# Two attentions on one core: the loads and splits of B's projection weights put in a set order, and B's gates loaded and made later

## The chip, the core and the metric

The kernel runs on one core of a Trainium2 chip. A core has five engines with instruction queues of their own: TensorE (PE, matrix products into PSUM), VectorE (DVE), ScalarE (ACT), GpSimd (POOL, which also issues DMAs) and SyncE (SP, which here only issues DMAs). Each engine works through its queue in order, and an instruction that waits holds up all behind it. Sixteen DMA engines move data. The time is the device time of the whole program in microseconds.

## What is computed

Two independent attentions over 2048 positions of 576 features, with 32 heads of 18, side by side in the output.

```python
# A: all heads share one k and one v
q = split_heads(x @ wq); k = x @ wk; v = x @ wv
a = merge(softmax(q @ k.T * 18**-0.5) @ v) @ wo

# B: four segments of 512, each causal within itself, plus a memory of the earlier ones
q, k, v = (split_heads(x @ w) for w in (wq, wk, wv))
g = sigmoid(beta)                       # one gate per head
for s in range(4):
    a_dot = softmax(causal(q[s] @ k[s].T * 18**-0.5)) @ v[s]
    a_mem = (phi(q[s]) @ M) / (phi(q[s]) @ z + 1e-6)      # phi(t) = t + 1 if t > 0 else exp(t)
    o[s] = g * a_mem + (1 - g) * a_dot
    M += phi(k[s]).T @ v[s]; z += phi(k[s]).sum()
b = merge(o) @ wo
```

## The kernel before

**Two stages.** The first (lines 146 to 558) makes all projections and writes q, k, v and the shifts of the softmax to DRAM. Then follows a branch on a flag (line 561), which all engines pass together. The second stage (from line 627) loops over the heads: scores, exponentials, products with v, output projection. Its order is written out by hand. The diff touches the first stage alone.

**Products in parts.** Every operand of a projection is split into a rounded high part and a remainder: `split_w` rounds a piece of raw weights `wr` into `wh` on ScalarE (L207) and subtracts on another engine to get `wl` (L208). For x the pair is L194 and L197/L198, mostly on VectorE. A projection (`proj`, L222) is 14 matmuls over five slices k of the 576 features: three products each for k = 0 to 3, two for k = 4, which holds only 64 features, loaded twice into both halves of the partitions (so its load is two DMAs).

**A's projections.** Four chunks c of 512 positions (L234), in each five tiles t in the order 4, 0, 1, 2, 3. Tile 4 holds the last heads' q, the shared k and v. For each tile, after its matmuls: for tile 4 a reduction km (DVE, L279), a copy vT of v's rows (ACT, L281), and four transposes by PE (L284); then for all tiles the magnitude AQ (ACT, L286), a split of the result into `qp` (ACT cast L111, DVE subtraction L112; three buffers), and a store to DRAM (SP). Beside it one tile of the next chunk's x is split (`nx[2](t)`; its raw tile `xr` has three buffers, loaded by SP), and, in chunks 2 and 3, one piece of B's weights is loaded and split (`load_wk`, L210).

**B's weights** come in 15 pieces of 128 rows. Five pieces of 648 columns (v's first half and part of k), five of 576 columns (the rest of k and v) and five of 504 columns (q of heads 0 to 27). The first ten are traced in A's chunks 2 and 3, the last five in the first loop of B's segment 0 (L430). Their targets `wBh` and `wBl` take the memory that held the raw x and weights of A's first chunks, so they can be written only when these have been read. Raw pieces stand in `wr`: two buffers in pool `pt`, and two in pool `p1`, which ends with A's part (L351).

**B's segments.** For each of four segments s: five tiles (L412) with projection, reduction kmB (L420), split (L111, L112), store, and, except in the last segment, a feature map `phi` (two ACT instructions L363 and L364, then DVE L366) that PE transposes (`natural`, L393); then the values (L454; ACT copies them to `vch` and issues their stores), then four tiles of q (L492). In segment 0 the projection of the first tile is made ahead (`ahead`, L329), before A's last small products. PE first needs the 504-column pieces at L492.

**The order on each engine** in this stage is laid at compile time by a planner. It follows the text of the program, except that it puts work ahead that it reckons to be ready sooner, by its own estimates of durations. `tc.issue_after(i)` queues what follows behind instruction i of the same engine. `tc.keep_in_program_order(i)`, used after the change, queues i behind the instruction of its engine that stands just ahead of it in the text. Neither waits for anything by itself.

**Gates and masks.** In chunk 2 (L303 to L325) POOL issues six small loads of masks, a store of ones and seven loads that spread beta over partitions; ACT and DVE make the gate `gt` and `omg` = 1 - gate from them. `gt` is first read in segment 1 (L408), `omg` in the second stage (L684), `sel` and `hmask` at L335 and L339.

Of the kernel before, what the change touches and what calls it, by code (L numbers as in the profile page):

```python
# [7 lines left out]
F32 = mybir.dt.float32  # L8
# [3 lines left out]
AF = mybir.ActivationFunctionType  # L12
ALU = mybir.AluOpType
# [55 lines left out]
def attention_pair_kernel(ctx, tc, a_xT, a_w, a_wo, b_xT, b_w, b_wo, b_beta, ident_d, hmask_d, bmask_d, cmask_d, sel_d, zmask_d, selx_d, sely_d, out):  # L69
# [76 lines left out]
    with ExitStack() as ph:  # L146
# [23 lines left out]
        def halves(k):  # L170
# [2 lines left out]
                return [(slice(0, 128), slice(128 * k, 128 * k + 128))]  # L173
            return [(slice(0, 64), slice(512, 576)), (slice(64, 128), slice(512, 576))]


        raw = [pw.tile([128, 5, 3 * D], F32, name=n) for n in ("wBl", "wBh")]
        XRAW = [(raw[0], CA), (raw[0], CA + C), (raw[1], 0)]

        def load_part(dst, w, c0, n, k, queue):  # L180
            for rows, src in halves(k):
                queue.dma_start(dst[rows], w[src, c0 : c0 + n])
# [5 lines left out]
        def load_xk(xh, xl, xT, c, k):  # L188
            if xT is a_xT and c < 3:
                xr = xraw(c, k)  # L190
            else:
                xr = px.tile([128, C], F32, name="xr", bufs=3)
                load_part(xr, xT, c * C, C, k, nc.sync)
            (nc.scalar.copy if xT is a_xT and c == 0 else nc.vector.tensor_copy)(xh[:, k], xr)  # L194
            engine = nc.gpsimd if xT is a_xT and (c, k) == (1, 3) else nc.vector
            if k < 4:
                return engine.tensor_tensor(xl[:, k], xr, xh[:, k].bitcast(F32), op=ALU.subtract)  # L197
            engine.tensor_tensor(xh[64:128, k], xr[64:128], xh[64:128, k].bitcast(F32), op=ALU.subtract)  # L198

        def next_x(xT, c):  # L200

# [3 lines left out]

        def split_w(wh, wl, wr, c0, n, k, engine):
            nc.scalar.copy(wh[:, k, c0 : c0 + n], wr)  # L207
            return engine.tensor_tensor(wl[:, k, c0 : c0 + n], wr, wh[:, k, c0 : c0 + n].bitcast(F32), op=ALU.subtract)  # L208
# [18 lines left out]
        wAl = p1.tile([128, 5, CA], F32R, name="wAl")  # L227


        TILES = (4, 0, 1, 2, 3)  # L230
        AQ = p1.tile([128, 5, S], BF, name="AQ")
        km = p1.tile([128, 4], F32, name="km")
        kAp = p1.tile([128, 1], F32, name="kAp")
        for c in range(NCH):  # L234
            ready = {}
            if c == 0:

                for k in range(5):
                    load_part(raw[0][:, k, :CA], a_w, 0, CA, k, nc.sync)
                    load_part(xraw(0, k), a_xT, 0, C, k, nc.sync if k > 1 else nc.scalar)  # L240
                for k in range(5):
                    load_part(xraw(1, k), a_xT, C, C, k, nc.sync)
# [19 lines left out]
                third = [nx[2](k) for k in range(5)][3]  # L262
            else:
                xh, xl = nx[:2]
                nx = next_x(a_xT, c + 1) if c < NCH - 1 else next_x(b_xT, 0)
                if c == 2:
                    wBl, wBh = (pw.tile([128, 5, 3 * D], F32R, name=n) for n in ("wBl", "wBh"))
            for t in TILES:
                M = 114 if t == 4 else 126
                if c == 0:  # L270
                    pj = ready[t]
                else:

                    nm, bufs = ("nd", 2) if c == 1 and t == 4 else ("pj", 4)
                    pj = ps.tile([128, C], F32, name=nm, bufs=bufs)
                    proj(pj[:M], wAh, wAl, xh, xl, 126 * t, M)
                R = RT[t]
                if t == 4:
                    nc.vector.tensor_reduce(km[:M, c : c + 1], pj[:M], axis=AX.X, op=ALU.max, apply_absolute_value=True)  # L279
                    vT = p1.tile([128, C], F32, name="vT", bufs=2)  # L280
                    nc.scalar.copy(vT[96:114], pj[96:114])  # L281
                    pv = ps.tile([128, 4, 128], F32, name="tr", bufs=1)
                    for i in range(4):
                        nc.tensor.transpose(pv[:, i, 0:DH], vT[96:114, 128 * i : 128 * i + 128], ident[96:114, 96:114])  # L284
                    nc.vector.tensor_copy(VAv[:, 4 * c : 4 * c + 4, 1:VW], pv[:, :, 0:DH])
                nc.scalar.activation(AQ[:R, t, c * C : c * C + C], pj[:R], AF.Abs)  # L286
                R2 = 90 if t == 4 else 126
                qp = split2(pt, pj[:R2], R2)
                store_parts(qp, 0, R, qA[c], H0[t], HT[t])
                if c == 0:  # L290
                    load_part(xraw(2, t), a_xT, 2 * C, C, t, nc.sync)
                if c:
                    nx[2](t)

                if c == 2:
                    with tc.issue_after(third.ins):
                        done = load_wk(wBh, wBl, b_w, 504, 648, t, p1 if t % 2 else pt)
                    first = done if t == 4 else first
                if c == 3:
                    load_wk(wBh, wBl, b_w, 2 * D, D, t, p1 if t % 2 else pt)  # L300
                if t == 4:
                    nc.sync.dma_start(kA[:, :, c * C : c * C + C], qp[72:90].bitcast(F32))
            if c == 2:  # L303
                nc.vector.memset(gt, 0.0)
                with tc.issue_after(first.ins):
                    nc.gpsimd.dma_start(hmask[:126], hmask_d)
                    nc.gpsimd.dma_start(bmask[:126], bmask_d)
                    nc.gpsimd.dma_start(sel[:114], sel_d)
                    nc.gpsimd.dma_start(zmask[:126], zmask_d)
                    nc.gpsimd.dma_start(selx[:126], selx_d)  # L310
                    nc.gpsimd.dma_start(sely, sely_d)
                    nc.gpsimd.dma_start(ones_d.rearrange("j (a b) -> (j a) b", b=128), onest)
                    for t in range(5):
                        lo, nh = H0[t], HT[t]
                        nc.gpsimd.dma_start(
                            gt[: RT[t], t : t + 1], b_beta[lo : lo + nh][:, None].to_broadcast([nh, DH])[:, :, None]
                        )
                    for t, lo, hi, n in ((5, 0, 28, 4), (6, 28, 32, 32)):
                        nc.gpsimd.dma_start(
                            gt[: n * (hi - lo), t : t + 1], b_beta[lo:hi][:, None].to_broadcast([hi - lo, n])[:, :, None]  # L320
                        )
# [3 lines left out]
                nc.vector.tensor_scalar(omg, gt, -1.0, 1.0, op0=ALU.mult, op1=ALU.add)  # L325
        nc.vector.memset(VAv[:, :, 0], 1.0)
        nc.vector.memset(VA[:, NKT * VW :], 0.0)
        xh, xl = nx[:2]
# [51 lines left out]
        for s in range(NSEG):  # L380
# [31 lines left out]
            for t in range(5):  # L412
# [123 lines left out]
            if s < NSEG - 1:  # L536
                for t in range(5):
# [572 lines left out]
```

## Time and profile before

| | us |
|---|---|
| median of three runs | 1466.66 |
| the three runs | 1465.25, 1466.66, 1470.65 |
| the profiled execution | 1469.55 |
| its span in the profile | 1466.6 |
| PE busy in the span | 1427.0 |
| ACT busy | 1194.6 |
| DVE busy | 1021.2 |
| POOL busy | 245.5 |

The span runs from the first to the last instruction. The page cuts it into 40 slices and gives each engine's busy share in tenths. The other views used below group waits by who ended them (in total, times, longest), list instructions in order of time (start, duration, engine, line, operation, what is written and read, and in brackets the idle time before it and what ended it), or sum up windows of time. A line such as L207 is a line of the kernel; a helper that several callers use has one line for all.

### The profile page before, as it was taken

Reading aid. Unit: us, or ns where it says so; the run is one execution under the profiler, and the core shown is the slowest. Engines: PE = TensorE matmul, PEld = TensorE weight load, DVE = VectorE, ACT = ScalarE, POOL = GpSimd, SP = SyncE. Lnnn points to the kernel's source line nnn. Section 1 sums busy time; section 2 is a strip of 40 time slices with the busy share of each in tenths; the row PEclk is TensorE's granted clock in tenths of the full one; section 3 lists DMA queues with packets and bytes.
Section 4 is the critical chain, followed back from the end, with each engine's and each line's share of the span. In section 5 each row is a group of like instructions: output and inputs, shape, how many; then the busy total and the mean of one; then the engine's idle time right before and its main releaser. Section 6 shows DMA issues by size and latency. Waiting matters only on the chain.

```text
span 1466.6 us, 40771 instructions
## 1 busy us (share of the span) xinstructions
PE 1427.0 (97%) x17540; PEld 847.8 (58%) x17540; DVE 1021.2 (70%) x1211; ACT 1194.6 (81%) x1429; POOL 245.5 (17%) x324
## 2 busy tenths in 40 slices
PE   9769999999999999999999999999999999999998
PEld 6658878774554555555555555555555555555566
DVE  6353744646766778887778787777778887887761
ACT  4323333249999999999999999999999999999970
POOL 2720000000233211603110151131111400100001
PEclk9979999999999999999999999999999999999999
DMA  8764544545755243533222251233113221210022
GB/s 261 216 201 130 179 147 136 181 166 157 201 143 167 80 143 127 150 111 103 85 73 74 95 168 53 76 109 104 49 33 124 85 72 33 70 42 17 17 75 84
DMA packets 86079, 166.33 MB, mean 113 GB/s; under 512 B 11872, under 2 KB 19673, under 8 KB 85718
## 3 DMA queue, kind: packets, MB, share of 16 engines
q1 hardware_dynamic: 79014, 152.87, 33.4%
q10 hardware_dynamic: 5216, 6.03, 1.3%
q0 software_dynamic: 1664, 4.78, 1.2%
q8 instruction: 138, 2.26, 0.7%
q14 instruction: 47, 0.39, 0.1%
HBM read 96.15 MB, written 67.49 MB: 112 GB/s over the span
## 4 chain that ended last, share of the span: by engine, by line
PE 65%; ACT 9%; issue 2%; DMA 1%; DVE 0%; POOL 0%; POOLq 0%; DVEq 0%; ACTq 0%
PE O L875 29%; PE E L827 19%; PE F L724 11%; ACT P L845 9%; PE E L836 3%; PE E L724 1%; PE O L724 1%; DMA rB<-sm 0%; DMA rb<-rB 0%; POOL o L711 0%; POOL P L850 0%; DVE W L842 0%; DVE q L807 0%; DVE sm L681 0%; DVE oe L884 0%
## 5 line engine op out<-in xcount | busy, mean ns | idle before, releaser
L845 ACT ACTIVATE P<-E 128x1024 f32<-128x1024 f32 (+1 forms) x800 | 788.0, 1077 | 15.1 <-PE E L827 11.8
L842 DVE COPY W<-E 128x1024 f32<-128x1024 f32 (+1 forms) x384 | 461.1, 1201 | 190.6 <-PE E L827 123.9
L875 PE MATMUL O<-P,VA 128*32 128x256 f32 x7936 | 509.7, 380 | 0.0
L845 ACT ACTIVATE P<-W 128x1024 f32<-128x1024 f32 (+1 forms) x384 | 434.0, 1130 | 1.5 <-DVE W L842 1.5
L875 PEld LDWEIGHTS O<-P,VA 128*32 128x32 f32 x7936 | 262.6, 110 | 146.6 <-issue 10.1
L827 PE MATMUL E<-stA,kstA 56*128 56x512 f32 x1920 | 331.0, 440 | 2.0 <-ACT P L845 1.3
L827 PEld LDWEIGHTS E<-stA,kstA 56*128 56x128 f32 x1920 | 154.6, 184 | 181.1 <-ACT P L845 121.7
L850 POOL TENSOR_SCALAR_AFFINE_SELECT P<-P 128x256 f32<-128x256 f32 (+1 forms) x192 | 94.2, 493 | 448.7 <-ACT P L845 415.9
L711 POOL TENSOR_TENSOR o<-o,rb 126x512 f32<-126x512 f32 (+1 forms) x40 | 58.1, 1458 | 433.3 <-PE F L724 144.0
L724 PE MATMUL F<-woB,o 126*32 126x192 f32 (+1 forms) x1920 | 127.6, 338 | 0.0
L807 DVE SCALAR_TENSOR_TENSOR q<-q,PD 128x1024 f32<-128x1024 f32 x96 | 117.7, 1226 | 0.0
L875 PE MATMUL O<-P,vseg 128*32 128x256 f32 (+2 forms) x1536 | 83.3, 348 | 2.0 <-POOL P L850 1.9
L112 DVE TENSOR_TENSOR qp<-pj,qp 126x512 fp32r<-126x512 f32 (+1 forms) x54 | 36.8, 686 | 64.0 <-ACT qp L111 63.9
L724 PEld LDWEIGHTS F<-woB,o 126*32 126x32 f32 (+1 forms) x1920 | 38.2, 108 | 70.8 <-issue 61.5
L724 PE MATMUL F<-woA,o 126*32 126x192 f32 (+1 forms) x1240 | 77.8, 338 | 0.6 <-DVE osb L749 0.6
L222 PE MATMUL pj<-xh,wBh 128*126 128x512 f32 x180 | 74.6, 415 | 0.0
L884 DVE COPY oe<-O 128x512 f32<-128x512 f32 x64 | 44.2, 691 | 41.1 <-PE O L875 39.5
L222 PE MATMUL pj<-xh,wBl 128*126 128x512 f32 x180 | 72.2, 401 | 0.0
L111 ACT CAST qp<-pj 126x512 fp32r<-126x512 f32 (+1 forms) x54 | 31.3, 583 | 49.8 <-DVE kmB L420 35.8
L836 PE MATMUL E<-stB 56*128 56x256 f32 (+3 forms) x512 | 62.5, 350 | 2.5 <-ACT P L845 2.0
L875 PEld LDWEIGHTS O<-P,vseg 128*32 128x32 f32 x1536 | 48.6, 110 | 28.1 <-issue 3.4
L222 PE MATMUL pj<-xl,wBh 128*126 128x512 f32 x144 | 59.5, 413 | 0.0
(178 smaller groups left out, 1384.8 us busy)
## 6 DMA issues: line engine op xcount, KB each, us to landing
stB<-kB SPq DMA_DIRECT2D x96, 144.0 KB
stB<-qB SPq DMA_DIRECT2D x32, 288.0 KB
stA<-qA SPq DMA_DIRECT2D x30, 288.0 KB
oA<-oe SPq DMA_DIRECT2D x32, 256.0 KB
oB<-oe SPq DMA_DIRECT2D x32, 256.0 KB
qA<-qp SPq DMA_DIRECT2D x16, 504.0 KB
kB<-qp SPq DMA_DIRECT2D x16, 504.0 KB
qB<-qp SPq DMA_DIRECT2D x16, 504.0 KB
```

The lines of the kernel that those rows point to most:

```text
L112: nc.vector.tensor_tensor(qp[:R, 1, :n], src, qp[:R, 0, :n].bitcast(F32), op=ALU.subtract)
L222: nc.tensor.matmul(dst, w[:, c0 : c0 + M], x, start=i == 0, stop=i == len(ops) - 1)
L711: steps = [lambda: v.tensor_tensor(o, o, rb, op=ALU.mult)]
L724: nc.tensor.matmul(dst[32 * j : 32 * j + 32], parts[ab, c][: RT[t], t, r0 : r0 + 32], wo[ab][: RT[t], t, c0 : c0 + n], start=start, stop=stop,
L807: steps.append(lambda a=a: v.scalar_tensor_tensor(q, q, a, p, op0=ALU.add, op1=ALU.mult))
L827: nc.tensor.matmul(e[:, j], kstA[rows, 128 * kt : 128 * kt + 128], st[rows, h, :], start=True, stop=True)
L836: nc.tensor.matmul(e[:, j, c0 : c0 + 512 - 128 * k], st[rows, 4 + h, ks], st[rows, h, 128 * k :], start=True, stop=True)
L842: nc.vector.tensor_copy(src[:, :, :n], e[:, :, :n])
L845: nc.scalar.activation(p[:, :, :n], src[:, :, :n], AF.Exp, scale=SCALE)
L850: nc.gpsimd.affine_select(diag, diag, pattern=[[0, 2], [0, m], [1, 128]], base=0, channel_multiplier=-1, compare_op=ALU.is_ge, fill=0.0)
L875: nc.tensor.matmul(o[32 * j : 32 * j + 32, q0 : q0 + n], v, p[:, j % 2, p0 : p0 + n], start=m == hf == 0, stop=last and hf == 1,)
L884: nc.vector.tensor_copy(osb, o)
```

## The change

The first ten pieces of B's weights are numbered in one list with the last five. The first four are loaded at the end of chunk 0's part of the program, and piece i+4 right behind the split of piece i, up to the tenth; piece 10 is loaded behind the split of piece 8. In segment 0 each tile splits a piece of the last five and then loads the next. Loads, roundings and subtractions are pinned in program order, so that ScalarE's rounding of a piece stands behind the cast of `qp` (or, for tile 4 of segment 0, the magnitude) of the same tile. The ten pieces alternate between the two pools; the last five all use the two buffers of `pt`. The masks are loaded behind the first four pieces, the gates behind the last piece, and the gates are made at the end of segment 0. `split_w`, `load_xk` no longer return an instruction.

```diff
-        def load_wk(wh, wl, w, c0, n, k, pool=pt):
-            wr = pool.tile([128, 648], F32, name="wr", bufs=2)[:, :n]
-            load_part(wr, w, c0, n, k, nc.gpsimd)
-            return split_w(wh, wl, wr, c0, n, k, nc.gpsimd)
+        WPARTS = [(504, 648, k) for k in TILES] + [(2 * D, D, k) for k in TILES] + [(0, 504, k) for k in range(5)]
+        wrs = {}
+
+        def load_wpart(i):
+            c0, n, k = WPARTS[i]
+
+            wrs[i] = (p1 if i % 2 and i < 10 else pt).tile([128, 648], F32, name="wr", bufs=2)[:, :n]
+            for rows, src in halves(k):
+                pin(nc.gpsimd.dma_start(wrs[i][rows], b_w[src, c0 : c0 + n]))
+
+        def split_wpart(i):
+            c0, n, k = WPARTS[i]
+            hi = wBh[:, k, c0 : c0 + n]
+            pin(nc.scalar.copy(hi, wrs[i]))
+            pin(nc.gpsimd.tensor_tensor(wBl[:, k, c0 : c0 + n], wrs[i], hi.bitcast(F32), op=ALU.subtract))
...
-                if c == 2:
-                    with tc.issue_after(third.ins):
-                        done = load_wk(wBh, wBl, b_w, 504, 648, t, p1 if t % 2 else pt)
-                    first = done if t == 4 else first
-                if c == 3:
-                    load_wk(wBh, wBl, b_w, 2 * D, D, t, p1 if t % 2 else pt)
+                i = 5 * (c - 2) + TILES.index(t)
+                if i >= 0:
+                    split_wpart(i)
+                    if i + 4 < 10 or i == 8:
+                        load_wpart(i + 4 if i < 8 else 10)
...
-            if c == 2:
-                nc.vector.memset(gt, 0.0)
-                with tc.issue_after(first.ins):
-                    nc.gpsimd.dma_start(hmask[:126], hmask_d)
...
-                    for t in range(5):
-                        lo, nh = H0[t], HT[t]
-                        nc.gpsimd.dma_start(
-                            gt[: RT[t], t : t + 1], b_beta[lo : lo + nh][:, None].to_broadcast([nh, DH])[:, :, None]
-                        )
...
-                nc.scalar.activation(gt, gt, AF.Exp, scale=-1.0)
-                nc.vector.tensor_scalar(gt, gt, 1.0, None, op0=ALU.add)
-                nc.vector.reciprocal(gt, gt)
-                nc.vector.tensor_scalar(omg, gt, -1.0, 1.0, op0=ALU.mult, op1=ALU.add)
+            if c == 0:
+                for i in range(4):
+                    load_wpart(i)
+                pin(nc.gpsimd.dma_start(hmask[:126], hmask_d))
...
                 if s == 0:
-                    load_wk(wBh, wBl, b_w, 0, 504, t)
+                    split_wpart(10 + t)
+                    if t < 4:
+                        load_wpart(11 + t)
...
+            if s == 0:
+                nc.vector.memset(gt, 0.0)
+                for t, lo, hi, n in [(t, H0[t], H0[t] + HT[t], DH) for t in range(5)] + [(5, 0, 28, 4), (6, 28, 32, 32)]:
+                    pin(
+                        nc.gpsimd.dma_start(
+                            gt[: n * (hi - lo), t : t + 1], b_beta[lo:hi][:, None].to_broadcast([hi - lo, n])[:, :, None]
+                        )
+                    )
...
+            if s == 0:
+                pin(nc.scalar.activation(gt, gt, AF.Exp, scale=-1.0))
+                pin(nc.vector.tensor_scalar(gt, gt, 1.0, None, op0=ALU.add))
+                pin(nc.vector.reciprocal(gt, gt))
+                pin(nc.vector.tensor_scalar(omg, gt, -1.0, 1.0, op0=ALU.mult, op1=ALU.add))
```

More of the change, by code (lines that the diff above doesn't have):

```diff
@@ L174, in halves @@
             return [(slice(0, 64), slice(512, 576)), (slice(64, 128), slice(512, 576))]
+        TILES = (4, 0, 1, 2, 3)
+        pin = tc.keep_in_program_order
         raw = [pw.tile([128, 5, 3 * D], F32, name=n) for n in ("wBl", "wBh")]
@@ L196, in load_xk @@
             if k < 4:
-                return engine.tensor_tensor(xl[:, k], xr, xh[:, k].bitcast(F32), op=ALU.subtract)
-            engine.tensor_tensor(xh[64:128, k], xr[64:128], xh[64:128, k].bitcast(F32), op=ALU.subtract)
+                engine.tensor_tensor(xl[:, k], xr, xh[:, k].bitcast(F32), op=ALU.subtract)
+            else:
+                engine.tensor_tensor(xh[64:128, k], xr[64:128], xh[64:128, k].bitcast(F32), op=ALU.subtract)
         def next_x(xT, c):
@@ L207, in split_w @@
             nc.scalar.copy(wh[:, k, c0 : c0 + n], wr)
[L208 to L213 removed]
+            engine.tensor_tensor(wl[:, k, c0 : c0 + n], wr, wh[:, k, c0 : c0 + n].bitcast(F32), op=ALU.subtract)
+        WPARTS = [(504, 648, k) for k in TILES] + [(2 * D, D, k) for k in TILES] + [(0, 504, k) for k in range(5)]
[10 more added lines that the diff above has]
+            pin(nc.gpsimd.tensor_tensor(wBl[:, k, c0 : c0 + n], wrs[i], hi.bitcast(F32), op=ALU.subtract))
         def proj(dst, wh, wl, xh, xl, c0, M):
@@ L261, in attention_pair_kernel @@
                             )
-                third = [nx[2](k) for k in range(5)][3]
+                for k in range(5):
+                    nx[2](k)
             else:
@@ new lines, in attention_pair_kernel @@
+            if c == 0:
+                for i in range(4):
+                    load_wpart(i)
+                pin(nc.gpsimd.dma_start(hmask[:126], hmask_d))
+                pin(nc.gpsimd.dma_start(bmask[:126], bmask_d))
+                pin(nc.gpsimd.dma_start(sel[:114], sel_d))
+                pin(nc.gpsimd.dma_start(zmask[:126], zmask_d))
+                pin(nc.gpsimd.dma_start(selx[:126], selx_d))
+                pin(nc.gpsimd.dma_start(sely, sely_d))
+                pin(nc.gpsimd.dma_start(ones_d.rearrange("j (a b) -> (j a) b", b=128), onest))
```

11 lines of the change are left out of this document (removed).

## The prediction

> **What bounds the kernel now.** I read the page's slices first: TensorE (PE) is busy in nearly every slice, and the two early ones where it is not are also those where its granted clock falls.
>
> ```profile
> PE   9769999999999999999999999999999999999998
> PEclk9979999999999999999999999999999999999999
> ```
>
> So I cut the first 140 us into windows at the places where PE stops and starts.
>
> ```profile
> 24.51:48.06 23.55, 23.55 (x105) 17.90 (x103) 14.93 (x27) 14.60 (x27) 13.65 (x16) 1.00 0.71 230
> 48.06:51.14 3.08, 0.00 (x1) 0.01 (x1) 2.38 (x5) 0.61 (x2) 3.08 (x6) 1.00 0.44 99
> 68.84:85.52 16.68, 0.00 (x0) 0.00 (x0) 4.87 (x8) 5.08 (x11) 10.14 (x12) 0.59 0.71 217
> 98.89:113.69 14.80, 14.80 (x79) 10.85 (x77) 11.78 (x28) 3.58 (x7) 0.35 (x1) 1.00 0.75 221
> 113.69:116.09 2.40, 0.00 (x0) 0.03 (x1) 2.33 (x5) 0.93 (x3) 0.00 (x0) 1.00 0.09 32
> 139.30:333.00 193.70, 192.72 (x1044) 151.57 (x1043) 102.16 (x230) 68.41 (x140) 1.05 (x3) 1.00 0.48 157
> ```
>
> The columns are the window and its length, busy time with instruction counts of PE, PE's weight loads, VectorE (DVE), ScalarE (ACT) and GpSimd (POOL), then granted clock, DMA share, GB/s. PE has two holes, 3.08 and 16.68 us, in the chunks of A's projections, a third of 2.40 us early in B's first segment, and none worth naming from 139 to 333 us. The loop over heads behind 333 us begins after a branch for all engines; the diff does not touch it. A hole ahead of the branch that closes moves everything behind it.
>
> Next, who ends the holes: the waits inside the large one, then the engines in order of time.
>
> ```profile
> PE tr L284 <- ACT vT L281: 16.7, 1, 16.7
> ACT wBh L207 <- DMA wr<-b_w: 14.2, 4, 4.9
> ```
> ```profile
> 42.67 0.73 ACT L207 CAST wBh<-wr 128x648 fp32r<-128x648 f32 x1 [3.06 <-DMA wr<-b_w]
> 50.50 0.58 ACT L281 COPY vT<-pj 18x512 f32<-18x512 f32 x1 [4.85 <-DVE km L279]
> 51.14 0.41 PE L284 MATMUL tr<-ident,vT 18*128 18x18 f32 x4 [3.08 <-ACT vT L281]
> 73.65 0.61 ACT L207 CAST wBh<-wr 128x504 fp32r<-128x504 f32 x1 [3.75 <-DMA wr<-b_w]
> ...
> 84.26 0.61 ACT L207 CAST wBh<-wr 128x504 fp32r<-128x504 f32 x1 [4.86 <-DMA wr<-b_w]
> 84.89 0.58 ACT L281 COPY vT<-pj 18x512 f32<-18x512 f32 x1
> 85.52 0.61 PE L284 MATMUL tr<-ident,vT 18*128 18x18 f32 x4 [16.69 <-ACT vT L281]
> ```
>
> PE needs a 0.58 us copy (vT) that stands on ACT's queue behind roundings of B's weights, and these stand waiting for loads (wr). The 504-wide pieces at 73.65 to 84.26 are not wanted by PE until B's q projections, yet they block ACT here. The small hole has the same root one step removed: ACT stood until 42.67 for a load, DVE's backlog behind it delayed the reduction km, and vT came at 50.50.
>
> **What the fifteen A tiles would cost without holes.** The projection matmuls alone, in the same windows:
>
> ```profile
> 24.51:98.89 74.38, 52.94 (x210) 40.71 (x211) 0.86 0.69 212
> 51.14:55.14 4.00, 3.66 (x9) 2.96 (x10) 0.57 0.76 195
> 55.14:68.84 13.70, 13.70 (x58) 10.23 (x57) 1.00 0.71 226
> 85.52:89.30 3.78, 3.23 (x8) 2.60 (x9) 0.54 0.60 152
> 89.30:98.89 9.59, 9.59 (x42) 7.66 (x42) 1.00 0.65 208
> ```
>
> At clock 1.00, 100 matmuls took 13.70 + 9.59 = 23.29 us, 0.233 each. So 210 need 48.9 us and four groups of transposes 0.41 each: 50.5. They took 74.38, so 24 us can be had at most. It adds up: 3.08 + 16.68 of holes, and behind each some 4 us at clocks 0.57 and 0.54, in which 9 and 8 matmuls took 7.78 instead of 3.96 us.
>
> **First part: ten pieces early, in order, each rounding behind the tile's own ACT work.** Four pieces are loaded at the start (as the queue did before), then piece i+4 as soon as GpSimd has subtracted piece i. One piece per tile of 14 x 0.233 = 3.26 us gives a load four tiles, 13 us. Off this goes what stands ahead of it on POOL:
>
> ```profile
> L208 POOL TENSOR_TENSOR wBl<-wr,wBh x9: 1234/1262/1489, 65.8 to 88.2; 128x504 fp32r<-128x504 f32 x5, 128x576 fp32r<-128x576 f32 x4
> DMA to landing us min/median/max: 2.9/4.9/5.4
> wr<-b_w POOLq DMA_DIRECT2D x4, 324.0 KB, 6.7
> wr<-b_w POOLq DMA_DIRECT2D x4, 288.0 KB, 10.0
> qA<-qp SPq DMA_DIRECT2D x15, 504.0 KB
> 10.00:15.00 5.00, 5.00 (x23) 3.96 (x22) 4.04 (x7) 2.57 (x4) 0.00 (x0) 1.00 1.06 304
> ```
>
> A cast, a subtraction and the issue take about 2.5 us; even the slowest group of loads (10.0) then lands in time. What may be late instead is bandwidth. Chunk 2 moves four stores of 504 KB, one of 288 and one of 72, five x tiles of 256 (128 x 512 x 4 bytes) and five pieces of 324: 5276 KB, in 16.7 us some 320 GB/s, over the best window shown (304). Behind that lies slack: stores may trail by the three qp buffers, and chunk 3 moves less. Bounds: 0 if the slack takes it all, 7 us if the engines move no more than the 230 GB/s of 24.51:48.06 (5.40 MB then take 23.5 us instead of 16.7). I take 2, nearer the lower end, since 304 is what they moved when asked for more. **Sum of the first part: -24 + 2 = -22 us.**
>
> **Second part: the last five pieces move into B's first segment.** Only the first of them is loaded ahead; each further load stands on POOL behind the subtraction of the piece before it, one in flight at a time. Price of a round, from the rows where it ran before:
>
> ```profile
> 74.35 1.23 POOL L208 TENSOR_TENSOR wBl<-wr,wBh 128x504 fp32r<-128x504 f32 x1 [1.51 <-ACT wBh L207]
> 75.88 0.56 POOL L182 DMA_DIRECT2D wr<-b_w  x1 [0.30 <-POOL wBl L208]
> ```
>
> From the cast at 73.65 to the issue at 75.88 are 2.23 us; landing adds 2.9 to 5.4 (the row above). I take 3.9, between the ends and below the median, because the landings come from the window 68.84:85.52 with a DMA share of 0.71, and B's segments run at 0.48 (139.30:333). A round is 6.1 us (5.1 to 7.6), against 3.26 of PE's tile: the chain, not PE, sets the pace of ACT. What it holds up, in the frame of before:
>
> ```profile
> 106.97 0.59 ACT L111 CAST qp<-pj 126x512 fp32r<-126x512 f32 x1 [6.80 <-issue]
> 122.98 0.59 ACT L111 CAST qp<-pj 126x512 fp32r<-126x512 f32 x1 [3.38 <-DVE kmB L420]
> 124.82 0.59 ACT L363 ACTIVATE ph_e<-pj 126x512 f32<-126x512 f32 x1
> 127.13 0.60 PE L393 MATMUL tr<-ident,qf 126*128 126x126 f32 x4
> ```
>
> The first rounding goes behind the cast at 106.97, at 107.6. Four rounds and 0.55 for the second half of the last load put the fifth at 132.5, done at 133.1. Queued behind it on ACT are the feature map (124.82 before), the copies of the values, and their stores; PE waits for the map with the transposes at 127.13, which come 2.3 us after the map begins: at 135.4, **+8.3 us**. Lower end: the planner puts the map ahead of the fifth rounding, so only the fourth (125.9) counts; from the tile's cast (122.98) to the transposes were 4.15 us before, so 130.6, +3.5. With that order and short landing, 0. Upper end: landing 5.4, fifth at 138.5, transposes at 141.4, +14.3. I take 8.3, as the rounding stands ahead of the map in the program text and needs, when the map becomes ready, only its load. No slow-clock loss is added: the 2.40 us hole at 113.69 with its slow matmuls is in the frame already.
>
> The Trainium skill's page "DMA: Bandwidth & Descriptors", section "Anatomy of one DMA — SWDGE (gpsimd) path", fits such a load as 2.0 us plus bytes over 436 GB/s, an estimate of 2.6 us for 252 KB; by it a round would be 4.8 us, the delay 3.2, and the time 1448. The rows above show 2.9 to 5.4, so they decide.
>
> **Third part: gates and masks.** Seven loads of gates leave POOL's queue ahead of the second five pieces and go behind the last load of the segment:
>
> ```profile
> L315 POOL DMA_DIRECT2D gt<-b_beta x5: 637/657/668, 46.4 to 48.8; - x5
> L325 DVE TENSOR_SCALAR omg<-gt x1: 1182/1182/1182, 63.8 to 63.8; 128x7 f32<-128x7 f32 x1
> L408 DVE TENSOR_SCALAR nm<-mm,gt x15: 741/750/752, 181.7 to 324.5; 126x512 f32<-126x512 f32 x12, 72x512 f32<-72x512 f32 x3
> ```
>
> They take 7 x 0.66 = 4.6 us of POOL, from about 134 to 139. Behind them can stand only the memset of vch, whose stores ACT issues; it waits for space alone and can go first: 0, at most 5 if it stays behind. The gate arithmetic (1.5 us on DVE, 1.2 of it one instruction, and less on ACT) now sits at the end of segment 0 and is first read at 181.7, in a stretch with PE busy 192.72 of 193.70: 0; uncovered it would be 1.5. The mask loads go out some 15 us sooner; the largest is 126 x 160 x 4 bytes, so all seven are at most 0.56 MB, 1.9 us at 304 GB/s, while PE works on data that has landed: 0.
>
> The five subtractions also move beside a DVE that is busy 11.78 of 14.80 us:
>
> ```profile
> 87.20 0.41 DVE L194 CAST xh<-xr 128x512 fp32r<-128x512 f32 x1
> 88.25 1.48 DVE L194 CAST xh<-xr 128x512 fp32r<-128x512 f32 x1
> ```
>
> The same cast took 1.07 us longer while POOL was subtracting (from 88.19). That is 0 to 2.1 us for two such casts on the path; I take 0, as the chain of loads is what PE waits for. The Trainium skill's "GPSIMD Engine Reference", section "1. Specifications", says that POOL shares its SBUF interfaces with VectorE and contends with its two-port modes; taken at its word this speaks against the move, and the sum would come out 2.1 us higher.
>
> **Sum.** -22 + 8.3 = -13.7 us. The profiled execution took 1469.55 us, span 1466.6 and 2.95 around it, so it would become 1455.9. It lies 2.9 above the median of the three runs, 1466.66; from the median the forecast is **1453.0**.
>
> **Rivals.**
> Full gain (0.27): the planner places the map ahead of the late roundings, or loads land at 2.9, so segment 0 loses 0 to 4.3 (five roundings at 5.1 end at 129.2). For it: the shortest landing lies at a round of 5.1 us. Against: one load in flight. Time 1466.66 - 22 + 2 = 1447, or 1443 if bandwidth costs nothing either. The Trainium skill's fit for loads, above, belongs to this case.
> Given back (0.20): landing 5.4 (+14.3) and bandwidth 4 us: -5.7, 1461. The diff "not doing what it says", with loads still late in chunks 2 and 3, lands here too: half of 24 and the 8.3 give 1463. For it: 320 against 304 GB/s.
> Slower (0.11): the chain of late pieces, with loads landing as the 288 KB group did. A landing of 10.0 makes a round of 12.2, the fifth rounding at 156.9, transposes at 159.8, +32.7, net +11: 1477. It decides from a landing of 7.3 us, where 22 us are given back, and is over 0.5% from 9.1. Against it: that group ran in a stretch of heavy stores, and B's segments run at less.
> The forecast itself (0.42) covers 1448 to 1459.
>
> **Range and chances.** No change means within 0.5%, 7.3 us, about what a measurement of this kernel can tell: 1459.3 to 1474.0. Forecast and full gain are faster, with 0.04 of the third case: 0.73. Same: 0.16. Slower: 0.11. The range takes the full gain to its lower bound, 1442, and the returned gain to 1466; the likeliest case alone is 1448 to 1459.
>
> **What would show it.** Right: vT's transposes in chunks 2 and 3 with no hole above 1 us and clock 1.00 from 25 to 75 us; no 504-wide rounding before B's first segment; that segment starting some 22 us earlier; in it roundings about 6 us apart, each ended by a load, and PE waiting for transposes of the feature maps. Wrong: loads of the first ten pieces still ending ACT's idle time, the map ahead of the roundings on ACT, or rounds much shorter or longer than 6 us.

## The result and the profile after

| | before | after |
|---|---|---|
| median of six runs, us | 1466.43 | 1449.18 |
| lowest to highest | 1465.22 to 1470.65 | 1447.41 to 1452.01 |
| ratio, 95% interval | | 0.988, 0.9865 to 0.9896 |
| profiled execution | 1469.55 | 1452.01 |
| its span | 1466.6 | 1450.0 |

The changed kernel is 17 us faster; 1453.0 had been forecast. The slices of the page of after, each a mean over some 36 us, show PE busy and its clock granted:

```profile
PE   9989999999999999999999999999999999999998
PEclk9999999999999999999999999999999999999999
```

Both profiles are now cut at the same places in the program: the first matmul of A's chunk 1, the first one with B's weights (`ahead`), and the transposes of segment 0's first feature map of q, `qf`. The last row ends where the loop over heads begins (its first exponential). The windows of before, with the columns of the prediction's:

```profile
24.74:98.89 74.15, 54.39 (x227) 41.99 (x226) 34.84 (x60) 30.99 (x58) 36.74 (x42) 0.86 0.69 212
98.89:127.13 28.24, 25.84 (x141) 20.71 (x140) 21.45 (x44) 10.46 (x21) 0.35 (x1) 0.94 0.62 186
127.13:333.01 205.88, 204.90 (x1135) 163.45 (x1134) 104.21 (x235) 71.90 (x152) 1.05 (x3) 1.00 0.47 154
```

The same of after, with one short window more:

```profile
22.96:75.25 52.29, 51.08 (x227) 39.67 (x226) 36.20 (x57) 27.90 (x51) 21.32 (x22) 1.00 0.83 273
75.25:109.69 34.44, 28.55 (x147) 22.81 (x146) 21.75 (x44) 13.50 (x27) 10.24 (x13) 0.90 0.69 213
84.94:88.29 3.35, 3.35 (x9) 2.62 (x8) 3.35 (x7) 1.10 (x2) 0.36 (x1) 0.51 0.61 192
109.69:315.26 205.57, 203.92 (x1126) 162.39 (x1127) 104.32 (x238) 72.30 (x152) 6.63 (x11) 1.00 0.48 154
```

A's tiles gained 74.15 - 52.29 = 21.9 us. The start of B lost 34.44 - 28.24 = 6.2. The rest of the stage is the same within 0.3. Two more pieces of the span's 16.6 us are not put down to the change: chunk 1 began 1.8 us earlier, which also differs between experiments with the same code up to there (the last section), and the loop over heads, whose code is the same, took 1134.7 instead of 1133.6. So 21.9 - 6.2 + 0.3 + 1.8 - 1.1 = 16.7, the 16.6 of the spans but for rounding.

What PE waits for in the first 110 us of after, in order of time:

```profile
63.41 0.41 PE L301 MATMUL tr<-ident,vT 18*128 18x18 f32 x4 [1.19 <-ACT vT L298]
83.11 1.26 PE L347 MATMUL nd<-AQ,kbdA 126*32 126x512 bf16 x20 [3.30 <-DVE kbdA L342]
97.33 0.62 PE L396 MATMUL tr<-ident,kf 126*128 126x126 f32 x4 [2.40 <-issue]
109.69 0.62 PE L396 MATMUL tr<-ident,qf 126*128 126x126 f32 x4 [0.19 <-DVE qf L369]
```

Of the holes of 3.08 and 16.68 us 1.19 is left. The one of 2.40 stands as before. New is the one of 3.30, ahead of the last small products of A, and what ended it is on DVE:

```profile
75.45 0.44 DVE L197 CAST xh<-xr 128x512 fp32r<-128x512 f32 x1 [1.20 <-PE pj L239]
79.42 0.43 DVE L197 CAST xh<-xr 128x512 fp32r<-128x512 f32 x1 [3.53 <-DMA xr<-b_xT]
82.63 0.15 DVE L339 COPY kAp<-mm 126x1 f32<-126x1 f32 x1
82.81 0.82 DVE L342 TENSOR_SCALAR kbdA<-hmask,kAp 126x32 bf16<-126x32 f32 x5
```

DVE stands 3.53 us at a cast of x for B's segment 1, which PE does not need before that segment. The planner had put it ahead of the 0.15 us copy kAp and of kbdA, for which PE waits. The matmuls behind the hole then ran at a clock of 0.51 (the window 84.94:88.29: nine in 3.35 us, 2.10 at full clock). So the 6.2 us are 3.5 of idle PE (34.44 - 28.55, less 28.24 - 25.84) and 2.7 of busy time, 1.25 of it in that slow window; six instructions more fell into the stretch.

The five late roundings, with the feature map of `qf` between the last two, in order of time on ACT:

```profile
87.24 0.62 ACT L229 CAST wBh<-wr 128x504 fp32r<-128x504 f32 x1
...
95.70 0.61 ACT L229 CAST wBh<-wr 128x504 fp32r<-128x504 f32 x1 [2.60 <-DMA wr<-b_w]
...
100.99 0.61 ACT L229 CAST wBh<-wr 128x504 fp32r<-128x504 f32 x1 [0.50 <-DMA wr<-b_w]
...
106.57 0.61 ACT L229 CAST wBh<-wr 128x504 fp32r<-128x504 f32 x1 [0.41 <-DMA wr<-b_w]
...
107.58 0.58 ACT L366 ACTIVATE ph_e<-pj 126x512 f32<-126x512 f32 x1
...
112.45 0.61 ACT L229 CAST wBh<-wr 128x504 fp32r<-128x504 f32 x1 [3.27 <-DMA wr<-b_w]
```

The rounds are 8.5, 5.3, 5.6 and 5.9 us, each ended by a load, as foreseen. But the map (107.58) stands ahead of the fifth rounding, and PE waited 0.19 us for it, 1.36 in a second profile of the same kernel.

### The profile page after: what moved, and what is told of

Its sections match the earlier page's. It is cut to its first block, busy times and chain, and to the rows that moved or that the text cites. A ratio compares the mean times of both kernels' runs of the same rounds, so it can differ in the third digit from the quotient of the medians.

```text
span 1450.0 us, 40761 instructions
## 1 busy us (share of the span) xinstructions
PE 1424.0 (98%) x17540; PEld 840.9 (58%) x17540; DVE 1023.9 (71%) x1211; ACT 1194.9 (82%) x1429; POOL 245.7 (17%) x324
## 4 chain that ended last, share of the span: by engine, by line
PE 64%; ACT 8%; DMA 3%; issue 2%; DVE 0%; POOL 0%; SPq 0%; DVEq 0%; POOLq 0%; ACTq 0%
PE O L893 30%; PE E L845 19%; PE F L742 11%; ACT P L863 8%; PE E L854 3%; PE E L742 1%; DMA sm<-oB 1%; PE O L742 1%; DMA rB<-sm 0%; DMA rA<-sm 0%; DMA stA<-qA 0%; DMA stB<-kB 0%; DMA stB<-qB 0%; DMA out<-osb 0%; DMA rb<-rB 0%
```

## The experiments

Two theories of the 6.2 us lost at the start of B. Theory A, the prediction's: the chain of late pieces, one load in flight. Theory B: DVE standing at a load of x ahead of A's last small products. Then a question about the 21.9 us gained: which part of the change brings them? The experiments ran in four groups, and each ratio is to the kernel before in the same group (medians 1466.89, 1467.44, 1465.53 and 1466.06). Profiles are of single executions.

**Two late pieces in flight.**

```diff
-                    if i + 4 < 10 or i == 8:
-                        load_wpart(i + 4 if i < 8 else 10)
+                    if i + 4 < 10 or i >= 8:
+                        load_wpart(i + 4 if i < 8 else i + 2)
...
-                    if t < 4:
-                        load_wpart(11 + t)
+                    if t < 3:
+                        load_wpart(12 + t)
```

> The changed kernel, with the second of the last five pieces also loaded ahead, so that two are under way in segment 0 instead of one. Theory A (as predicted: the chain of the late pieces holds ScalarE, and through it PE, by about 6 us in segment 0): 4 to 6 us below the changed kernel, 1443 to 1445. Theory B (the loss in segment 0 is VectorE standing at a load of x for segment 1 in front of A's shifts, 3.3 us of hole and 2 us of slow clock behind it): at most 2 us, 1447 to 1449, with the hole ahead of L347 still there.

Measured: 1450.34, ratio 0.9895 (0.9875 to 0.9914): no gain on 0.988. Its windows:

```profile
22.87:78.09 55.22, 52.69 (x228) 40.81 (x226) 32.48 (x57) 28.05 (x51) 21.11 (x22) 0.97 0.84 267
78.09:111.09 33.00, 27.88 (x147) 22.64 (x146) 23.71 (x44) 13.74 (x28) 12.27 (x16) 0.90 0.69 215
```

Segment 0's start gets 1.4 us shorter, with 2.02 us of hole ahead of A's last products instead of 3.30, and A's tiles 2.9 longer. That the piece loaded one step sooner is in the way of chunk 3's loads is likely, but was not tried. The 4 to 6 us of theory A are not there: the chain alone is not what the 6.2 us hang on.

**x of segment 1 behind A's shifts.** `shifted` is the instruction that makes kbdA.

```diff
-                    nx[2](t)
-                    if t == 3:
-                        nx[2](4)
+                    with tc.issue_after(shifted.ins):
+                        nx[2](t)
+                        if t == 3:
+                            nx[2](4)
```

> The changed kernel, with VectorE's conversions of segment 1's x queued behind the five small products for A's shifts (L342). Theory A: no change, 1448 to 1450. Theory B: the hole of 3.3 us ahead of L347 goes and with it 2 us of slow clock; since the roundings in segment 0 stay as late as they are, PE may wait for them longer: 2 to 5 us below the changed kernel, 1444 to 1447.

Measured: 1447.23, ratio 0.9866 (0.9843 to 0.9889). In order of time:

```profile
79.68 0.62 PE L347 MATMUL nd<-AQ,kbdA 126*32 126x512 bf16 x8
96.46 1.07 PE L396 MATMUL tr<-ident,kf 126*128 126x126 f32 x4 [2.37 <-DVE kf L369]
```

The hole of 3.30 us is gone, so what made it is shown: DVE's stand ahead of kbdA. The stretch got only 2.3 us shorter (32.14), as another wait of 2.37 us opened, for a feature map of k. The median is 2 us below after, but the intervals of the two ratios overlap.

**Both edits together.**

> The two edits together. Theory A: as with two pieces in flight alone, 1443 to 1445. Theory B: 5 to 7 us below the changed kernel, 1442 to 1444, more than the sum of the two edits alone, as each alone uncovers the other's wait.

Measured: 1445.75, ratio 0.9854 (0.9833 to 0.9876), the lowest of all kernels here.

```profile
22.95:78.68 55.73, 52.66 (x227) 40.86 (x226) 33.69 (x57) 27.80 (x51) 21.39 (x22) 0.97 0.83 264
78.68:108.44 29.76, 26.51 (x144) 20.89 (x143) 22.28 (x44) 13.54 (x28) 12.21 (x16) 0.94 0.75 241
```

The start of B takes 29.76, 4.7 less than in after, where the edits alone took off 1.4 and 2.3. That each wait had covered part of the other would fit; single profiles do not show it. A's tiles again give back 3.4. The medians put it 3.4 us below after, less than the 5 to 7 expected, and the intervals just overlap; against x_behind_shift alone no difference is shown.

**Why that x is late: half of q's stores.** In chunks 2 and 3 only the high part of q is stored, 2.4 MB less (not 4.6, as the expectation says). The low parts are left out; two copies of 1152 KB between DRAM tensors in segment 1 fill their place with the high parts.

```diff
-                store_parts(qp, 0, R, qA[c], H0[t], HT[t])
+                if c < 2:
+                    store_parts(qp, 0, R, qA[c], H0[t], HT[t])
+                else:
+                    nc.sync.dma_start(
+                        qA[c][H0[t] : H0[t] + HT[t], :, 0, :].rearrange("h d t -> (h d) t"), qp[:R, 0].bitcast(F32)
+                    )
...
+                if s == 1:
+                    for c_ in (2, 3):
+                        nc.sync.dma_start(qA[c_][:, :, 1, :], qA[c_][:, :, 0, :])
```

> The changed kernel, storing only the high parts of q in A's chunks 2 and 3 (4.6 MB less in the stretch; the low parts are filled by a copy between DRAM tensors in segment 1, so A's scores for these chunks are computed from other numbers). If the load of x for segment 1 is late because the DMA engines are full (theory B with bandwidth): the holes of 1.2 us before vT's transposes and of 3.3 us ahead of L347 shrink to under 1 us each, 3 to 6 us less, 1443 to 1446. If it is late because SP issues it late: the holes stay, 1448 to 1450.

Measured: 1452.7, ratio 0.9911 (0.9892 to 0.993).

```profile
80.81 1.26 PE L352 MATMUL nd<-AQ,kbdA 126*32 126x512 bf16 x20 [0.82 <-DVE kbdA L347]
```

The hole shrinks from 3.30 to 0.82 and the stretch to 30.5, so q's stores are what makes x late. Whether by their traffic or by their place on SP's queue the run does not tell, as it changes both. From 58 to 80 us the DMA engines move 221 GB/s instead of 279. And the load in question (by the order of the loads) goes out at 65.29 instead of 73.92. In after its buffer was free at 70.10, but on SP it stood behind two stores, one of which waited 2.4 us for DVE's low part, and then it took 5.5 us to land.

The time gained nothing, and the interval lies a little above that of after. From `qf` to the loop over heads the profile took 207.6 us against 205.6, and the trace shows the experiment's own copies there: they stand on SP's queue from 203.6 to 224.5 us, so the stores of k that begin at 208.1 in after begin at 224.6. ACT waits 3.43 us for such a store to free a buffer, and PE then 1.20 and 0.67 us for feature maps.

**The last five pieces pinned in the kernel before, nothing else.**

```diff
-                    load_wk(wBh, wBl, b_w, 0, 504, t)
+                    wr = pt.tile([128, 648], F32, name="wr", bufs=2)[:, :504]
+                    load_part(wr, b_w, 0, 504, t, nc.gpsimd)
+                    tc.keep_in_program_order(nc.scalar.copy(wBh[:, t, 0:504], wr))
+                    nc.gpsimd.tensor_tensor(wBl[:, t, 0:504], wr, wBh[:, t, 0:504].bitcast(F32), op=ALU.subtract)
```

> The kernel before, with one edit: the rounding of the last five pieces is pinned behind ScalarE's work on the same tile of segment 0; the loads of the first ten, the masks and the gates stay as they were. If the place of these five made the large hole: it shrinks from 16.7 to under 4 us, the small one of 3.1 stays, segment 0 gives 4 to 7 us back: 1454 to 1460. If the late loads of the first ten made it: the hole keeps over 10 us, 1462 to 1467.

Measured: 1461.03, ratio 0.9951 (0.9929 to 0.9974), 6.4 us. The large hole falls from 16.7 to 7.55 us, between the two cases expected, and no 504-wide rounding is left in chunk 3. What holds the rest, in order of time:

```profile
57.86 0.21 ACT L322 ACTIVATE gt<-gt 128x7 f32<-128x7 f32 x1 [7.57 <-DMA wr<-b_w]
58.45 0.58 ACT L111 CAST qp<-pj 126x512 fp32r<-126x512 f32 x1
63.74 0.54 SPq L182 DMA_DIRECT2D xr<-b_xT  x1
67.43 0.32 SPq L116 DMA_DIRECT2D qA<-qp  x1
67.80 1.51 SPq L182 DMA_DIRECT2D xr<-b_xT  x2
73.87 0.43 DVE L194 CAST xh<-xr 128x512 fp32r<-128x512 f32 x1 [5.50 <-DMA xr<-b_xT]
75.56 0.61 PE L284 MATMUL tr<-ident,vT 18*128 18x18 f32 x4 [7.55 <-ACT vT L281]
```

ACT stands 7.57 us at the exponential of the gates, and a cast of qp stands behind it. The stores on SP wait for the casts, the loads of x stand behind the stores (the two halves of this tile, by the order of the loads, at 63.74 and 67.80), and DVE waits for x ahead of the reduction km, so vT is late. The profile names a load of wr at the first row; the instruction reads `gt`. The kernel before has the same stand:

```profile
51.60 0.57 ACT L111 CAST qp<-pj 90x512 fp32r<-90x512 f32 x1
61.12 0.21 ACT L322 ACTIVATE gt<-gt 128x7 f32<-128x7 f32 x1 [8.95 <-DMA wr<-b_w]
62.17 1.83 ACT L207 CAST wBh<-wr 128x576 fp32r<-128x576 f32 x3
```

Of the gates' last two loads and of all seven the view of the tile `gt` in the same trace says

```profile
L319 POOL DMA_DIRECT2D gt<-b_beta x2: 637/700/764, 49.5 to 50.0; - x2
DMA to landing us min/median/max: 2.9/6.3/10.9
```

(durations in ns, then the first and last start.) The last load went out at 50.0; with the longest landing that is 60.9, right ahead of 61.12. So I read the wait as the gates' own; where the gates are put back, below, the profile itself names their loads.

**The changed kernel without the pins of the last five.** They are loaded and rounded where the planner puts them.

```diff
-                    if i + 4 < 10 or i == 8:
-                        load_wpart(i + 4 if i < 8 else 10)
+                    if i + 4 < 10:
+                        load_wpart(i + 4)
...
-                    split_wpart(10 + t)
-                    if t < 4:
-                        load_wpart(11 + t)
+                    wr = pt.tile([128, 648], F32, name="wr", bufs=2)[:, :504]
+                    load_part(wr, b_w, 0, 504, t, nc.gpsimd)
+                    split_w(wBh, wBl, wr, 0, 504, t, nc.gpsimd)
```

> The changed kernel, with the last five pieces loaded and split as before the change (not pinned, so the planner puts their roundings into chunk 3, but behind the last copy of vT). Theory: with vT ahead of them they no longer make a hole at the transposes; ScalarE waits for loads at the end of chunk 3 instead and PE follows at the start of segment 0: within 5 us of the changed kernel, 1445 to 1454. Rival (these five need the pin to keep the gain): over 1457.

Measured: 1455.92, ratio 0.991 (0.9873 to 0.9946), 6.7 above after by the medians and between the two cases expected. The intervals overlap, but its four runs (from 1452.95) all lie above those of after (to 1452.01).

```profile
90.86 1.47 PE L347 MATMUL nd<-AQ,kbdA 126*32 126x512 bf16 x12 [9.27 <-DVE kbdA L342]
```

The roundings go ahead again; the wait moves from vT to A's last products.

**The gates back at the end of chunk 2, loads and arithmetic.** The first block below is moved from segment 0, the second from its end.

```diff
+            if c == 2:
+                nc.vector.memset(gt, 0.0)
+                for t, lo, hi, n in [(t, H0[t], H0[t] + HT[t], DH) for t in range(5)] + [(5, 0, 28, 4), (6, 28, 32, 32)]:
...
+                nc.scalar.activation(gt, gt, AF.Exp, scale=-1.0)
+                pin(nc.vector.tensor_scalar(gt, gt, 1.0, None, op0=ALU.add))
...
-            if s == 0:
-                nc.vector.memset(gt, 0.0)
...
-            if s == 0:
-                pin(nc.scalar.activation(gt, gt, AF.Exp, scale=-1.0))
```

> The changed kernel, with the gates loaded and made at the end of chunk 2, as before the change. Theory: four pieces of lead cover the 4.6 us of issues on POOL: within 2 us of the changed kernel, 1447 to 1451. Rival (the gates' loads held the weights up and moving them is part of the gain): 3 to 6 us more, 1452 to 1455.

Measured: 1455.12, ratio 0.9924 (0.9894 to 0.9954), 5.9 above after by the medians: the rival.

```profile
75.74 0.21 ACT L327 ACTIVATE gt<-gt 128x7 f32<-128x7 f32 x1 [7.54 <-DMA gt<-b_beta]
```

**The gates' loads alone back:** of the diff just shown the first block alone, the arithmetic stays late. Beside it runs the changed kernel once more, unaltered.

> The changed kernel with only the seven loads of the gates back at the end of chunk 2; the gates are still made at the end of segment 0. If it was ScalarE's exponential, standing 7.5 us for the gates' loads in the middle of chunk 3, that cost the 5 to 6 us seen with both back: within 2 us of the changed kernel run beside it. If it was the issues on POOL or the traffic of these loads: 4 to 6 us above it, and a load of x or of weights lands late in chunk 3.

> The changed kernel itself, as the yardstick for the run beside it: 1449, within 2. Theory B says that its segment 0 again shows a hole of 2 to 4 us ahead of L347 and a first late rounding about 8 us behind its load's issue or less; theory A nothing else.

Measured: 1456.17, ratio 0.9937 (0.9922 to 0.9952), and for the changed kernel 1449.31, ratio 0.9888 (0.987 to 0.9906): the seven loads, 0.5 KB or less each, cost 6.9 us even when nothing reads them soon. In the changed kernel it is thus the loads that cost, and ACT's stand at the exponential adds nothing to be seen. A window of gates_loads_back:

```profile
70.00:72.00 2.00, 2.00 (x10) 1.59 (x10) 0.00 (x0) 0.53 (x1) 1.68 (x3) 1.00 0.85 43
```

and in order of time, the same kernel:

```profile
63.61 4.63 POOL L323 DMA_DIRECT2D gt<-b_beta  x7
76.72 0.43 DVE L197 CAST xh<-xr 128x512 fp32r<-128x512 f32 x1 [7.40 <-DMA xr<-b_xT]
89.37 2.32 PE L355 MATMUL nd<-AQ,kbdA 126*32 126x512 bf16 x20 [6.17 <-DVE kbdA L350]
```

From 70 to 72 us the DMA engines are busy 0.85 of the time and move 43 GB/s; 0.63 of their time goes to 29 packets of POOL's queue with 0.00 MB in all. DVE stands 7.40 us at a load of x, issued on SP, not POOL: by the order of the loads it went out at 65.24 and took 11.5 us, and the same one in after went out at 62.05 and took 6.0 at most. DVE falls behind, and PE's hole ahead of A's last products is 6.17 instead of 3.30. The Trainium skill's page "DMA: Bandwidth & Descriptors", section "Rules for kernel authors", says that a transfer whose last dimension isn't contiguous goes as one descriptor for each element; these loads put one element of 4 bytes into each partition, 816 in all, so I read them as such a case. The 29 packets without a megabyte fit; how many descriptors there were no view shows. The issues also hold POOL's queue for 4.63 us; how much of the 6.9 is that was not tried apart.

**Two pieces of lead instead of four.**

```diff
-                    if i + 4 < 10 or i == 8:
-                        load_wpart(i + 4 if i < 8 else 10)
+                    if i + 2 < 10 or i == 8:
+                        load_wpart(i + 2 if i < 8 else 10)
...
-                for i in range(4):
+                for i in range(2):
```

> The changed kernel with the first ten pieces loaded two ahead instead of four. A piece then has two tiles, 6.5 us, less 2.5 for cast, subtraction and issue, against landings of 5.7 to 8.2 us in the changed kernel: ScalarE waits for loads again by 1 to 4 us a piece and PE has holes at the transposes, 3 to 12 us more, 1452 to 1461. If only the order mattered and not the lead: within 1 us.

Measured: 1451.29, ratio 0.9874 (0.9839 to 0.9908): not to be told from after, and not the 3 to 12 us more that were expected. ACT does wait for loads of the first ten again, 6.3 us in four waits in A's tiles (none in after), and PE's holes are 2.39 and 4.58 us instead of 1.19 and 3.30. So the lead of four may be worth a us or two, but the times do not show it.

**From the other end: the kernel before with the gates late.** The loads and the arithmetic of the gates stand as in the change; nothing else is changed.

```diff
-                nc.vector.memset(gt, 0.0)
...
-                    for t in range(5):
-                        lo, nh = H0[t], HT[t]
...
-                nc.scalar.activation(gt, gt, AF.Exp, scale=-1.0)
...
+            if s == 0:
+                nc.vector.memset(gt, 0.0)
...
+            if s == 0:
+                tc.keep_in_program_order(nc.scalar.activation(gt, gt, AF.Exp, scale=-1.0))
```

> The kernel before with only the gates moved as in the change (their seven loads and their arithmetic, from the end of chunk 2 to behind segment 0); B's weights and roundings as they were. Theory that the seven small loads clog the transfers at the end of chunk 2 (the windows of gates_back and gates_loads_back: 34 to 96 GB/s while the engines of the DMA are busy) whatever the order of the roundings: the weights that ScalarE waits for in chunk 3 land sooner, the large hole of 16.7 us shrinks by 4 to 8 us, the time is 1458 to 1463. Rival, that the gates only matter where the pins have made the late chunks tight: before, they land while ScalarE is behind anyway, and the time is 1465 to 1468.

Measured: 1463.98, ratio 0.9976 (0.9958 to 0.9994). It lies between the two cases expected, and the hole shrank by 6 us while the time fell by 2. In order of time:

```profile
68.10 0.61 ACT L207 CAST wBh<-wr 128x504 fp32r<-128x504 f32 x1 [5.73 <-DMA wr<-b_w]
75.62 0.61 ACT L207 CAST wBh<-wr 128x504 fp32r<-128x504 f32 x1 [4.45 <-DMA wr<-b_w]
79.80 0.61 ACT L207 CAST wBh<-wr 128x504 fp32r<-128x504 f32 x1 [3.57 <-DMA wr<-b_w]
81.07 0.61 PE L284 MATMUL tr<-ident,vT 18*128 18x18 f32 x4 [10.55 <-ACT vT L281]
```

Without the stand at the gates ACT stands at the late pieces instead, and 10.55 us of hole remain. The loads of weights that had followed the gates' loads land sooner: the four whole 576-column pieces (288 KB) took 10.0 us (median) in the kernel before and 6.5 here.

**The kernel before with the gates late and the last five pinned:** the edit just shown and that of the last five pinned in the kernel before, together.

> The kernel before with the gates moved and the last five roundings of wr pinned in segment 0, and nothing else: the first ten pieces stay where the planner put them. By the first theory it gets what last_five_pinned (1461.0) and the gates' 6 to 7 us give together: 1452 to 1456, with the hole of 7.55 us ahead of the last part of the rows of v under 3 us and the one of 3.08 us left. If it also reaches the changed kernel's 1449, the first ten pins and the lead are worth nothing. By the rival it stays at 1459 to 1462.

Measured: 1452.7, ratio 0.9911 (0.9891 to 0.9932).

```profile
50.62 0.61 PE L284 MATMUL tr<-ident,vT 18*128 18x18 f32 x4 [3.90 <-ACT vT L281]
69.31 0.42 PE L284 MATMUL tr<-ident,vT 18*128 18x18 f32 x4 [0.96 <-ACT vT L281]
```

The large hole is gone. Alone the two edits give 2.1 and 6.4 us, together 13.4. Only the small hole is left, and it is the first ten pieces': two of their roundings stand ahead of that vT, after 4.63 us of waiting for a load. With the rest of the change, as in after, the time is 1449, some 3 to 4 us lower, though the intervals overlap (0.9865 to 0.9896 there).

## Why the prediction came out right

**The first part, -22: right in size, incomplete in cause.** A's stretch gained 21.9. The ceiling of 24, from the holes and the slow clock behind them, was sound: the stretch took 52.3 us at a clock of 1.00, against the 50.5 reckoned without holes, and the 2 us for bandwidth were near. The step that failed is the root: "504-wide pieces ... block ACT here" was true and half of it. The other half was the gates, 8.95 us of stand on ACT at 61.12, in the trace of before all the time. With the gates gone but the pieces there the hole is 10.55; with the pieces gone but the gates there, 7.55; with both gone, 0.96. Whether it was ACT's stand or the traffic of the gates' loads was not taken apart in the kernel before; in the changed one the loads alone cost the whole. The order, pins and lead of the first ten bring about 3 us, which is not clear of the noise, and only the small hole. One reading was off as well: the clock in the page's slices falls only in the second of the two early ones (9, then 7); that it fell behind both holes the windows show.

**The second part, +8.3: a near number for a wrong reason.** 6.2 were measured. The rounds were as worked out in their sum (mean 6.3 against 6.1; the fifth rounding 25.2 us behind the first against 24.95), but that is one of 8.5 and three of 5.3 to 5.9. The step that failed is the order on ACT: the map was placed ahead of the fifth rounding, the variant that the prediction priced at +3.5, and the chain then cost PE 0.19 us (1.36 in the second profile). What the 6.2 us were in the profile is mostly the stand of DVE at x, which no part had, and the slow clock behind it; without that stand 2.3 us came back, and with two pieces in flight as well 4.7. The load of x came late there because of q's stores, as half of them showed: A's traffic is pressed into less time (273 GB/s for 52 us against 212 for 74), and the load stands behind stores on SP. How much each does is open. The prediction let the stores trail and did not ask which load stands behind them. That 6.2 lies near 8.3 is luck.

**The third part, 0: wrong.** It priced the gates' move by the durations of the instructions, 4.6 us of POOL and 1.5 of DVE, and asked only what they would cost in the new place. What they held up in the old one, the transfers of others and ACT's order, is worth 6 to 7 us in the changed kernel. A sign of it stood in the prediction's own row: the 288 KB pieces that took 10.0 us went out right behind the gates' loads. The sum did not suffer, since the ceiling of the first part already held this gain. A change with the pins but not the gates would have been given the same 1453; it took 1455.1 (the gates back), so the 6 us would have turned a forecast 4 us too slow into one 2 us too fast.

**The rivals.** Full gain, 1447, came nearer to 1449.2 than the forecast did, and its premise, the map ahead of the late rounding, came true; yet 6.2 us were lost, by another wait. Against the span that was forecast, 1466.6 - 13.7 = 1452.9, the profile's 1450.0 is 3 us shorter: 2.1 of this term and 1.8 of the early chunk 1, less 1.1 in the loop over heads, and small change. Slower, by landings over 7.3 us all along, was not seen: behind the first, of 8.5, all rounds were under 6, landing included. The signs named as right held, but for a hole of 1.19 us instead of under 1 and PE's waits, the longer of which were at the transposes of a map of k and for DVE. One of the signs named as wrong came as well: the map ahead of a rounding on ACT.

## What to carry to other kernels

Before pricing a move, look at what stands before the moved instruction in the trace: a 0.2 us instruction with 9 us of idle time ahead of it holds up its whole queue. Where two waits end at the same place, take each away alone and then both: 2.1 and 6.4 us apart were 13.4 together. Small loads that spread single elements belong where no large load is waited for. And an experiment that thins out one engine's work also moves its queue: look at what else the edit changes before naming one cause.

## What the hardware showed unexpectedly

- With seven loads of at most 0.5 KB under way the DMA engines were 0.85 busy at 43 GB/s for 2 us, 0.63 for 29 packets of these loads' queue; in that run each took 6.1 to 11.2 us to land, and 3.1 to 6.2 us in after, where they go out behind segment 0's last weights (44 GB/s from 115 to 120 us).
- Chunk 1 begins at 22.9 to 23.0 us in some profiles (after, twice; both edits together; gates late and last five pinned) and at 24.5 to 24.9 in others (before; gates late alone; two pieces of lead), though the code ahead of it is much the same. The first four matmuls of A show about half of it, in order of time, before

```profile
6.69 2.05 PE L255 MATMUL pj<-xh,wAh 128*114 128x512 f32 x4 [1.13 <-ACT wAh L207]
```

and after

```profile
6.64 1.19 PE L271 MATMUL pj<-xh,wAh 128*114 128x512 f32 x4 [1.08 <-ACT wAh L212]
```

The same four took 2.05 us once and 1.19 the other time. The Trainium skill's page "TensorE: Matmul & The Clock Gate", section "Part 1: The HAM clock gate", says that the number of slow matmuls at the start differs from run to run, as the clock's window runs freely; that fits, but was not tried.
- The loop over heads took 1134.7 us in the first profile of the changed kernel and 1128.9 in its second: a few us between two single executions say nothing about an edit.
